# The gate of the first 1024 tokens: partial sums by GpSimd instead of TensorE

## The chip, the cores and the metric

One core of one Trainium2 chip runs the kernel. The metric is the device time of one execution in microseconds, as the median of several runs. The engines are TensorE (PE; its weight loads are PEld), VectorE (DVE), ScalarE (ACT), GpSimd (POOL) and SyncE (SP, which here only issues DMAs). "Line" and "L" numbers are lines of the kernel's source.

## The reference

The kernel computes a gated mix of an attention block and a mixture of 64 experts, for 2048 tokens of 1024 features in fp32. The gate is one number for each token, the sum over all features of x times a weight vector:

```python
def reference(A_x, A_wqkv, A_wo, B_x, B_w_q, B_k1, B_k2, B_u, B_v, gate_w):
    ...
    x = A_x
    g = _sigmoid((x * gate_w).sum(-1, keepdims=True))
    a = _A_ref(x, A_wqkv, A_wo)
    b = _B_ref(x, B_w_q, B_k1, B_k2, B_u, B_v)
    return g * a + (1 - g) * b
```

The attention needs the queries and keys, x times the first 2048 columns of wqkv. The change lies in this first stage, in the part that also sums x times gate_w.

## The kernel before

x comes transposed: features on partitions, in eight row blocks of 128 (kc from 0 to 7), tokens along the free dimension. The stage of queries and keys goes in two passes of 1024 tokens, the second half of the tokens first (pass 0), and in units of 128 output columns of queries and of keys each. x and the weights are fp32; for TensorE every operand is split in a rounded upper part (ScalarE, a copy into fp32r) and the remainder (VectorE, a subtraction), and every product is three matmuls.

The first unit of a pass is computed plainly, all the others with seven products in place of eight (Strassen's method in Winograd's form). For this x of a pass is seen as four blocks: B11 and B12 are kc 0 to 3 of the first and second 512 tokens, B21 and B22 are kc 4 to 7. In the plain unit of pass 0 (the loop over kc) each kc is loaded, split (split_x, recorded at L95 on ScalarE and L96 on VectorE) and multiplied by twelve matmuls (plain_mm, L291). Its four results lie in PSUM banks 7, 0, 1 and 2.

The code after the loop makes the sums of the seven products: x_sum (L153, VectorE) computes T1 = B12 - B11, T3 = B22 - B12, T2 = B22 - T1 and T4 = B21 - T2. Each result is written over a block that is no longer needed: T1 over B11, T3 over B12, T2 over B22, T4 over B21. x_hi and x_lo (recorded at L136 and L139) split them. The split of T3 is put where the raw B22 and T2 lay (tile xh2), so it follows x_lo of T2; that of T4 is put where B11 and B12 lay (tile xh1), so it follows x_lo of T3. evac takes a result out of a bank: a copy of its upper part, the remainder, a square with accumulation (L247, ScalarE, written in place into the bank) and two DMAs from GpSimd's queue. The squares and DMAs of one evac are put off to the next one (run_late).

unit(1) then issues the products P1, P5, P6, P2, P7, P3, P4 (product, L303), each with its bank in turn from a rotation of six (bank_at(prod_no % 6), which plain_banks sets to 3), and the adds between them (L513, VectorE). Functions put into hooks run after the product that they name. Every engine executes its instructions in the order in which the code issues them; engines wait for each other only where one needs what another writes, or writes what another still reads. Tiles with bufs=1 have one buffer: a new tile of that name waits until all readers of the old one are through, DMAs included.

The gate of pass 0 is gate_mm: a column of gw, 128x1, as the weights and x itself as the data, 256 tokens at a time, into rows 0, 32, 64 and 96 of bank 5, summed over kc in PSUM. It stands in the loop ahead of kc 4 and of kc 6, 16 matmuls each. gate_out copies the four rows into zs (a tile named u2; ScalarE, L198) and stores them in ZD by four DMAs from GpSimd's queue. Pass 1 does the same at its own place. The names u2, u4, u7 and c1 are also those of the working tiles of each unit.

Of the kernel before, what the change touches and what calls it, by code (L numbers as in the profile page):

```python
# [9 lines left out]
F32 = mybir.dt.float32  # L10
# [3 lines left out]
OP = mybir.AluOpType  # L14
# [5 lines left out]
KC = D // 128  # L20
HC = KC // 2
# [10 lines left out]
def gated_mha_peer_kernel(ctx, tc, xT, wqkv, wv, wo, wq, k12, ug, v, out):  # L32
# [8 lines left out]
    nc = tc.nc  # L41
# [23 lines left out]
    ones = const.tile([128, 32], F32, name="ones")  # L65
# [5 lines left out]
    gw = const.tile([128, KC, 1], F32, name="gw")  # L71
# [3 lines left out]
    def dma(dst, src, queue=nc.sync):  # L75
        a, b = (ap.bitcast(F32) if ap.dtype == F32R else ap for ap in (dst, src))
        return queue.dma_start(a, b)
# [37 lines left out]
    def bank_at(i):  # L115
        return ps1.tile([128, 512], F32, name=f"bk{i}")
# [3 lines left out]
    ev = Pool("ev", bufs=3)  # L120
# [5 lines left out]
    X, AW, XR, wraw = {}, {}, {}, {}  # L126
# [14 lines left out]
    def x_hi(p, name):  # L141
        X[name] = x_parts(PASS[p][name], None, xp)
        hi_of(X[name], XR[name])
# [26 lines left out]
    def load_x(p, kc, pieces=1):  # L170
        rows, t0 = slice(kc * 128, (kc + 1) * 128), TOK0[p]
        if kc < HC:
            n = 1024 // pieces
            for i in range(pieces):
                dma(XR["ra"][:, kc, i * n:(i + 1) * n], xT[rows, t0 + i * n:t0 + (i + 1) * n])
        else:
            for i, name in enumerate(("B21", "B22")):
                dma(XR[name][:, kc - HC, :], xT[rows, t0 + i * 512:t0 + (i + 1) * 512])

    def x_raw_at(kc, c):  # L180
        n, c = divmod(c, 512)
        return XR[f"B{1 + kc // HC}{1 + n}"][:, kc % HC, c:c + 256]

    pz = []

    def gate_mm(kcs):
        if kcs[0] == 0:
            pz[:] = [bank_at(5)]
        for kc in kcs:
            for q in range(4):  # L190
                nc.tensor.matmul(pz[0][32 * q:32 * q + 1, :256], gw[:, kc, :], x_raw_at(kc, 256 * q),  # L191
                                 start=(kc == 0), stop=(kc == KC - 1))

    def gate_out(p):
        zs = ev.tile([128, 512], F32, name="u2", bufs=1)
        for q in range(4):
            row = slice(32 * q, 32 * q + 1)
            nc.scalar.activation(zs[row, :256], pz[0][row, :256], AF.Copy)  # L198
            c = TOK0[p] + 256 * q
            dma(ZD[:, c:c + 256], zs[row, :256], nc.gpsimd)  # L200


    def load_w(u):
        t = wr.tile([128, 2, KC, 128], F32, name="wraw")
        for w in range(2):
            dma(t[:, w], wqkv[w * 8 + CHUNK[u]].rearrange("p (k m) -> p k m", k=KC))
        wraw[u] = raw_quarters(t)
# [73 lines left out]
    b0, prod_no = {}, [0]  # L281
# [6 lines left out]
    def plain_mm(w, n, kc, i, first=False, last=False):  # L288
        ki, k = divmod(kc, HC)
        a, b = ((0, 0), (0, 1), (1, 0))[i]  # L290
        nc.tensor.matmul(b0[w, n], AW[PLAIN[w, ki]][a][:, k, :], X[f"B{ki + 1}{n + 1}"][b][:, k, :],  # L291
                         start=first, stop=last)

    FACTORS = dict(P1=("A11", "B11"), P2=("A12", "B21"), P3=("S4", "B22"), P4=("A22", "T4"),
                   P5=("S1", "T1"), P6=("S2", "T2"), P7=("S3", "T3"))
# [22 lines left out]
    def load_wqs():  # L318
        while wq_no[0] < min(fold_no[0] + 2, 32):
            load_wq(wq_no[0])  # L320
            wq_no[0] += 1
# [53 lines left out]
    def split_w0(k0, k1):  # L375
        ki, k = divmod(k0, HC)
        for w in range(2):
            hi, lo = AW[PLAIN[w, ki]]
            split(hi[:, k:k + k1 - k0], lo[:, k:k + k1 - k0], w0[:, w, k0:k1])

    def split_x(kc):
        ki, k = divmod(kc, HC)
        for n in range(2):
            hi, lo = X[f"B{ki + 1}{n + 1}"]
            split(hi[:, k, :], lo[:, k, :], XR[f"B{ki + 1}{n + 1}"][:, k, :])
# [28 lines left out]
    for kc in range(KC):  # L414
        if kc:
            split_x(kc)
        if kc in (1, 2):
            split_w0(2 * kc, 2 * kc + 2 if kc == 1 else KC)
        if kc + 4 < KC:
            load_x(0, kc + 4)  # L420
        if kc == 3:
            load_w(1)
        if kc == 4:
            load_wqs()
        if kc == HC:
            gate_mm(range(HC))
        if kc == KC - 2:
            gate_mm(range(HC, KC))
        order = [(w, n, i) for w in range(2) for i in range(3) for n in range(2)]
        if kc == 0:  # L430
            order = [(w, n, i) for n in range(2) for pair in ((0, 2), (1,)) for w in range(2) for i in pair]
        if kc == KC - 1:
            order = [(w, n, i) for w in range(2) for n in range(2) for i in range(3)]
        for w, n, i in order:
            plain_mm(w, n, kc, i, kc == 0 and i == 0, kc == KC - 1 and i == 2)


    def plain_evac(u, w, n):
        evac(w, CHUNK[u], TOK0[u // KC] // 512 + n, b0[w, n], b0[w, n])

    hooks = {}
# [17 lines left out]
    w_lo(1, "S2")  # L459
    w_lo(1, "A12")  # L460
    plain_evac(0, 1, 0)
    gate_out(0)
    x_hi(0, "T3")
    x_lo(0, "T3")
    plain_evac(0, 0, 1)
# [6 lines left out]
    w_lo(1, "S4")  # L472
    x_lo(0, "T4")
    hooks[1, "P1"] = [(plain_evac, 0, 1, 1), (w_parts, 1, "A22"), (run_late,)]
    hooks[1, "P5"] = [(plain_evac, 0, 0, 0)]
    dma(WPD[:, :, 448:], ug.rearrange("p (k m) -> p k m", k=KC)[:, :, :64], nc.gpsimd)
    load_w(2)
    fold()
# [117 lines left out]
    plain_banks(1)  # L596
    load_wqs()
    gate_mm(range(KC))
    nxt = KC + 1

# [311 lines left out]
    class Halves:  # L912
# [9 lines left out]
                       P5=("S1", "T1"), P6=("S2", "T2"), P7=("S3", "T3"))  # L922
# [847 lines left out]
```

## Time and profile before

| | |
|---|---|
| median of 3 runs | 1818.84 us (1818.75 to 1820.33) |
| the profiled execution | 1820.62 us, span 1818.8 us |
| granted TensorE clock, mean | 0.999 |
| busy: PE, DVE, ACT, POOL | 1810.3, 1470.1, 1314.7, 230.7 us |
| the loop over kc with the gate in it | up to about 35.6 us from the span's start |
| unit 1, first product to the end of its fold | 37.5 to 58.7 us |

Times in the profile's rows are from the start of the span. A row of the timeline has the start in us, the time taken in us, the engine, the line, the operation, output <- input, how many instructions are merged in it, and in brackets how long the engine had been idle and what ended that. A row of the grouped views has the count, then busy us and mean ns of one, then the idle time ahead of them. "min/median/max" rows are ns, except for DMAs, whose time to landing is in us. A row of the table by stretches has the stretch, its length, then busy us and count for PE, PEld, DVE, ACT and POOL, the granted clock, the DMA engines' share and GB/s. The chain of waits is the work that ended last, followed back from the end.

### The profile page before, as it was taken

The page shows a single profiled execution, that of the slowest core. Times are in us where ns is not written, and L with a number is a line of the kernel's source. Part 1 is how long each engine was busy: PE and PEld are TensorE (multiplying, and loading weights), DVE is VectorE, ACT ScalarE, POOL GpSimd, SP SyncE. Part 2 cuts the span into 40 slices and gives each one's busy share as a digit, 9 for nine tenths or more (in the row PEclk, how much of TensorE's full clock was granted, in tenths as well). Part 3 has the DMA queues.
Part 4 walks back from the last instruction along what each step waited for, and adds up shares of the span by engine and source line. Part 5 has one row for each costly group of instructions (what it writes and reads, how often), then busy time and mean ns, then how long its engine had stood idle before and what let it go on. Part 6 is the DMA issues. An engine that isn't in the chain of part 4 may idle for free.

```text
span 1818.8 us, 26381 instructions
## 1 busy us (share of the span) xinstructions
PE 1810.3 (100%) x10057; PEld 1096.5 (60%) x10057; DVE 1470.1 (81%) x1273; ACT 1314.7 (72%) x1720; POOL 230.7 (13%) x355
## 2 busy tenths in 40 slices
PE   9999999999999999999999999999999999999999
PEld 6777777788888644444444444444444444447887
DVE  7865966689977888888888888888888888897874
ACT  5545644532343599999999999999999999994221
POOL 1222222244101100000000000000000000000000
PEclk9999999999999999999999999999999999999999
DMA  7888698660267878777787877888787787878641
GB/s 259 278 288 263 226 280 304 197 226 14 81 221 239 240 161 179 155 171 167 162 186 166 180 172 167 175 175 183 162 180 172 158 179 167 184 166 291 228 157 58
DMA packets 116913, 346.28 MB, mean 190 GB/s; under 512 B 16001, under 2 KB 49185, under 8 KB 95729
## 3 DMA queue, kind: packets, MB, share of 16 engines
q1 hardware_dynamic: 87320, 196.05, 36.4%
q0 software_dynamic: 28160, 146.35, 34.9%
q10 hardware_dynamic: 1304, 2.17, 0.3%
q8 instruction: 80, 1.31, 0.3%
q14 instruction: 49, 0.39, 0.1%
HBM read 171.76 MB, written 72.36 MB: 134 GB/s over the span
## 4 chain that ended last, share of the span: by engine, by line
PE 99%; DMA 0%; ACT 0%; SPq 0%; issue 0%; DVE 0%; DVEq 0%; ACTq 0%
PE ring L1322 29%; PE o L1343 26%; PE bk L303 15%; PE pa L965 7%; PE bk L965 6%; PE bk L726 5%; PE bk L291 2%; PE bk L984 2%; PE bk L342 2%; PE ring L1356 1%; PE pa L1525 1%; PE pa L1532 1%; PE bk L191 0%; DMA xh<-in_xT 0%; PE bk L359 0%; ACT P L1332 0%
## 5 line engine op out<-in xcount | busy, mean ns | idle before, releaser
L1332 ACT ACTIVATE P<-ring 128x1024 f32<-128x1024 f32 (+2 forms) x1031 | 913.0, 983 | 13.3
L1372 DVE TENSOR_TENSOR acc<-acc,P 128x2048 f32<-128x2048 f32 x319 | 731.0, 2291 | 74.5 <-ACT P L1332 48.5
L1343 PE MATMUL o<-P,V 128*32 128x512 f32 x3840 | 464.8, 599 | 0.0
L1322 PE MATMUL ring<-Q,K 98*128 98x512 f32 x1024 | 271.7, 407 | 0.1
L1322 PE MATMUL ring<-z,z 98*128 98x512 f32 x1020 | 270.4, 407 | 0.6 <-ACT accd L1332 0.6
L1322 PEld LDWEIGHTS ring<-Q,K 98*128 98x128 f32 x1024 | 182.1, 188 | 143.6 <-ACT P L1332 73.5
L1322 PEld LDWEIGHTS ring<-z,z 98*128 98x128 f32 x1020 | 181.4, 188 | 142.4 <-ACT P L1332 72.3
L1343 PEld LDWEIGHTS o<-P,V 128*32 128x32 f32 x3840 | 98.8, 109 | 223.5 <-issue 214.5
L1365 POOL DMA_DIRECT2D accd<-P x96 | 82.3, 858 | 935.4 <-ACT P L1332 327.4
L1370 DVE TENSOR_TENSOR acc<-P,P 128x2048 f32<-128x2048 f32 x32 | 73.4, 2292 | 72.6 <-ACT P L1332 72.6
L303 PE MATMUL bk<-xh,A 128*128 128x512 f32 x336 | 82.8, 396 | 0.0
L303 PE MATMUL bk<-xh,S 128*128 128x512 f32 x336 | 81.3, 393 | 0.0
L303 PE MATMUL bk<-xl,S 128*128 128x512 f32 x336 | 80.1, 391 | 0.0
L136 ACT ACTIVATE hi<-u 128x512 fp32r<-128x512 f32 x42 | 26.6, 632 | 72.2 <-DVE u L513 37.2
L303 PEld LDWEIGHTS bk<-xh,A 128*128 128x128 f32 x336 | 62.1, 188 | 23.8 <-issue 5.0
L1375 DVE TENSOR_TENSOR acc<-acc,accd 128x2048 f32<-128x2048 f32 x32 | 73.1, 2284 | 0.0
L303 PEld LDWEIGHTS bk<-xl,S 128*128 128x128 f32 x336 | 62.8, 188 | 16.3 <-issue 2.5
L965 PE MATMUL pa<-woh,acc 128*128 128x512 f32 x224 | 72.5, 389 | 0.0
L303 PEld LDWEIGHTS bk<-xh,S 128*128 128x128 f32 x336 | 62.4, 188 | 14.5 <-issue 1.7
L1332 ACT ACTIVATE accd<-ring 128x1024 f32<-128x1024 f32 (+2 forms) x64 | 62.3, 1033 | 1.8 <-PE ring L1322 1.7
L513 DVE TENSOR_TENSOR u<-u,bk 128x512 f32<-128x512 f32 x70 | 46.6, 683 | 11.3 <-PE bk L303 10.1
L730 ACT ACTIVATE xu<-bk 128x64 f32<-128x64 f32 x16 | 3.6, 222 | 61.2 <-PE bk L726 61.2
(305 smaller groups left out, 2209.7 us busy)
## 6 DMA issues: line engine op xcount, KB each, us to landing
accd<-P POOLq DMA_DIRECT2D x96, 1024.0 KB, 7.7
wqt<-in_wq SPq DMA_DIRECT2D x64, 512.0 KB
wraw<-in_wqkv SPq DMA_DIRECT2D x28, 512.0 KB
kdh<-hi POOLq DMA_DIRECT2D x32, 256.0 KB, 5.9
kdl<-lo POOLq DMA_DIRECT2D x32, 256.0 KB, 7.1
qdh<-hi POOLq DMA_DIRECT2D x32, 256.0 KB, 6.3
qdl<-lo POOLq DMA_DIRECT2D x32, 256.0 KB, 6.3
z<-kdh SPq DMA_DIRECT2D x32, 256.0 KB
```

The lines of the kernel that those rows point to most:

```text
L291: nc.tensor.matmul(b0[w, n], AW[PLAIN[w, ki]][a][:, k, :], X[f"B{ki + 1}{n + 1}"][b][:, k, :], start=first, stop=last)
L303: nc.tensor.matmul(ps, a[i][:, k, :], b[j][:, k, :], start=(k == 0 and i == j == 0), stop=(k == HC - 1 and i == 1))
L513: nc.vector.tensor_tensor(out=out, in0=a, in1=b, op=OP.add)
L726: nc.tensor.matmul(ps, x_part(a, t // 4, kc)[:, tok], b, start=first, stop=last)
L965: nc.tensor.matmul(ps, self.a[a][i][:, k, :], self.b[b][j][k], start=(not first and k == 0 and i == j == 0), stop=(k == HC - 1 and i == 1))
L1322: on_ring(nc.tensor.matmul(ring[:, i, :], K[:98, kt * 128:(kt + 1) * 128], Q[:98, qc * 512:(qc + 1) * 512], start=True, stop=True), i)
L1332: on_ring(nc.scalar.activation(P[h, kt][:, q0 * 512:(q0 + m) * 512].rearrange("p (a m) -> p a m", a=m), ring[:, i:i + m, :], AF.Exp, scale ...
L1343: nc.tensor.matmul(O[h][32 * qc:32 * qc + 32, :], Vt[g][:, kt, 32 * j:32 * j + 32], p[:, qc * 512:(qc + 1) * 512], start=(kt == 0), stop=( ...
L1365: nc.gpsimd.dma_start(ACCD[h], P[h, kt], accum_op=OP.add)
L1370: nc.vector.tensor_add(ACC[h], P[h, 0], P[h, kt])
L1372: nc.vector.tensor_add(ACC[h], ACC[h], P[h, kt])
L1375: nc.vector.tensor_add(ACC[h], ACC[h], ACCD[h])
```

## The change

The gate of pass 0 is no longer a sum of 32 small matmuls in the loop. For each kc and each half n of the tokens GpSimd multiplies the 128x512 block of x by the column of gw (tensor_scalar), and from kc 1 on adds the product to a running sum of 128x512 in fp32 (tensor_tensor). The two running sums are tiles named u4 and u7, the product is a tile named u2. Issued in the loop ahead of the matmuls of each kc, that is 16 tensor_scalar and 14 tensor_tensor. What is left is the sum over the 128 partitions: gate_fold, four matmuls with a column of ones, into the next bank of the rotation. It and gate_out are moved from the code ahead of unit 1 into unit 1, behind P5. Pass 1 still uses gate_mm.

```diff
     pz = []
 
+    def gate_acc(kc, n):
+        x = XR[f"B{1 + kc // HC}{1 + n}"][:, kc % HC, :]
+        if kc == 0:
+            pz.append(ev.tile([128, 512], F32, name=("u4", "u7")[n], bufs=1))
+            nc.gpsimd.tensor_scalar(pz[n], x, gw[:, kc, :], None, op0=OP.mult)
+        else:
+            t = ev.tile([128, 512], F32, name="u2", bufs=1)
+            nc.gpsimd.tensor_scalar(t, x, gw[:, kc, :], None, op0=OP.mult)
+            nc.gpsimd.tensor_tensor(out=pz[n], in0=pz[n], in1=t, op=OP.add)
+
...
+
+    def gate_fold():
+        parts = pz[:]
+        pz[:] = [bank_at(prod_no[0] % 6)]
+        prod_no[0] += 1
+        for q in range(4):
+            nc.tensor.matmul(pz[0][32 * q:32 * q + 1, :256], ones[:, :1], parts[q // 2][:, q % 2 * 256:q % 2 * 256 + 256],
+                             start=True, stop=True)
...
-        if kc == HC:
-            gate_mm(range(HC))
-        if kc == KC - 2:
-            gate_mm(range(HC, KC))
+        for n in (0, 1) if kc < HC else (1, 0):
+            gate_acc(kc, n)
...
     plain_evac(0, 1, 0)
-    gate_out(0)
     x_hi(0, "T3")
...
-    hooks[1, "P5"] = [(plain_evac, 0, 0, 0)]
+    hooks[1, "P5"] = [(plain_evac, 0, 0, 0), (gate_fold,), (gate_out, 0)]
```

## The prediction

> **What bounds the kernel now.** I read the page's engine shares and chain first, then the chain of waits of the first 70 us, where the change lies, then the timeline there, and last every row of the trace in which GpSimd (POOL) does arithmetic.
>
> ```profile
> PE 1810.3 (100%) x10057; PEld 1096.5 (60%) x10057; DVE 1470.1 (81%) x1273; ACT 1314.7 (72%) x1720; POOL 230.7 (13%) x355
> PE 99%; DMA 0%; ACT 0%; SPq 0%; issue 0%; DVE 0%; DVEq 0%; ACTq 0%
> ```
>
> TensorE is the bound: 99% of the chain. A microsecond that leaves its queue comes off the end, and a microsecond that it newly waits is added to the end, since it has no slack later to give it back. So the whole question is when TensorE gets through the stage around the change.
>
> ```profile
> 10.71 10.00 PE bk L291 x35
> 20.70 1.84 PE bk L191 x32
> 22.54 5.66 PE bk L291 x24
> 28.20 1.84 PE bk L191 x32
> 30.04 5.66 PE bk L291 x24
> 35.70 1.85 PE bk L342 x16
> 37.56 19.31 PE bk L303 x84
> ```
>
> L291 is the plain first unit, L191 the gate's matmuls, L342 the folds, L303 the seven products. The gate stands on the chain with 2 x 1.84 = 3.68 us. That is what the change can take from TensorE. It puts back gate_fold, four matmuls that appear as eight records: 8 x 1.84/32 = 0.46 us. Seen from TensorE alone: -3.2 us.
>
> **What VectorE does there.** The adds replace reads by TensorE with reads by GpSimd, and the blocks of x that they read are overwritten soon after by x_sum (L153): T1 goes into B11, T3 into B12, T2 into B22, T4 into B21. So these sums now wait for GpSimd. The timeline has them, and the steps that lead on to the third product, P6:
>
> ```profile
> 9.51 1.15 ACT L95 ACTIVATE xh<-xh 128x512 fp32r<-128x512 f32 x2 [2.84 <-DMA xh<-in_xT]
> 10.17 1.29 DVE L96 TENSOR_TENSOR xh<-xh,xh 128x512 fp32r<-128x512 f32 x2 [2.75 <-ACT xh L95]
> 22.58 2.29 DVE L153 TENSOR_TENSOR xh<-xh 128x2048 f32<-128x2048 f32 x1 [1.77 <-PE bk L191]
> 31.19 2.29 DVE L153 TENSOR_TENSOR xh<-xh,xh 128x2048 f32<-128x2048 f32 x1
> 36.80 2.29 DVE L139 TENSOR_TENSOR xh<-xh,xh 128x2048 fp32r<-128x2048 f32 x1
> 37.93 1.56 ACT L198 ACTIVATE u<-bk 1x256 f32<-1x256 f32 x4
> 38.58 1.98 POOL L77 DMA_DIRECT2D zd<-u  x4 [30.93 <-ACT u L198]
> 39.51 1.92 ACT L136 ACTIVATE xh<-xh 128x2048 fp32r<-128x2048 f32 x1
> 41.95 0.60 ACT L247 ACTIVATE bk<-bk 128x512 f32<-128x512 f32 x1
> 42.88 2.68 PEld L303 LDWEIGHTS bk<-xh,S 128*128 128x128 f32 x12
> 45.60 2.68 PEld L303 LDWEIGHTS bk<-xl,A 128*128 128x128 f32 x12
> 46.13 0.58 ACT L247 ACTIVATE bk<-bk 128x512 f32<-128x512 f32 x1
> 51.61 0.68 DVE L513 TENSOR_TENSOR u<-c,bk 128x512 f32<-128x512 f32 x1
> 53.76 2.68 PEld L303 LDWEIGHTS bk<-xh,A 128*128 128x128 f32 x12
> ```
>
> T1 starts at 22.58 and T2 at 31.19; the lower part of T2 (L139) ends at 39.09; P6 starts at 42.88, P2 at 45.60, P4 at 53.76. VectorE leads TensorE by 3.8 us at P6 and no more. From T2's start to the end of its lower part it takes 7.9 us without a pause: T2, the lower part of S1, T4, S2, the lower part of T2.
>
> **GpSimd's work.** It is 16 tensor_scalar and 14 tensor_tensor, each 128x512. The prices:
>
> ```profile
> 6.31 1.34 POOL L326 TENSOR_TENSOR kpad<-kraw 128x14 f32<-128x14 f32 x4 [2.94 <-DMA kraw<-in_k]
> L740 POOL TENSOR_TENSOR eq<-eq,ranks 128x512 f32<-128x512 f32 x16 | 20.6, 1289 | 14.2 <-DVE eq L739 14.2
> L324 POOL MEMSET kpad<- 128x256 f32 x1 | 0.4, 355 | 0.0
> ```
>
> The tensor_tensor has a row of its own size: 1.29 us. No tensor_scalar of GpSimd is in the trace. It has one large input; I bound it below by the memset of half the elements (0.36 us) and above by the two-input row (1.29 us), and take twice the memset, 0.71 us. The Trainium skill, GPSIMD Engine Reference, Engine selection, calls one-input work on GpSimd roughly line-rate and two-input work about half VectorE's speed; read as VectorE's pace, that would put this operation near 0.69 us, and the sum would stay within half a microsecond. No run here shows it yet.
>
> T2 needs the adds through block 7 of B22: two operations for kc 0, four each for kc 1 to 6, two for kc 7, which is 15 tensor_scalar and 13 tensor_tensor. That is 15 x 0.71 + 13 x 1.29 = 27.4 us on GpSimd, against 23.5 us between its last kpad operation (7.65) and the present T2. Already this is too long. But GpSimd isn't alone:
>
> ```profile
> L762 POOL TENSOR_TENSOR pq<-eq,p x32: 651/662/2703, 381.3 to 462.9; 128x256 f32<-128x256 f32 x32
> 381.22 2.28 DVE L96 TENSOR_TENSOR xh<-rx,xh 128x2048 fp32r<-128x2048 f32 x1
> 381.33 3.29 POOL L762 TENSOR_TENSOR pq<-eq,p 128x256 f32<-128x256 f32 x2 [0.52 <-DVE p L755]
> L750 DVE TENSOR_TENSOR eq<-eq,mm x16: 426/1058/1069, 380.0 to 460.5; 128x256 f32<-128x256 f32 x16
> 392.32 1.29 POOL L740 TENSOR_TENSOR eq<-eq,ranks 128x512 f32<-128x512 f32 x1 [0.35 <-DVE eq L739]
> 392.82 1.06 DVE L750 TENSOR_TENSOR eq<-eq,mm 128x256 f32<-128x256 f32 x1
> ```
>
> A GpSimd operation of 0.66 us that starts 0.1 us after a two-input VectorE operation takes 2.70 us and ends 0.53 us after it (381.33 + 2.70 = 384.03, against 383.50). A VectorE operation of 0.43 us that starts under a GpSimd one takes 1.06 us and ends 0.27 us after it (393.88 against 393.61). So the later one waits for the earlier; about 0.13 to 0.16 us of each is all that overlaps. In the stage of the change nearly every VectorE operation is such a two-input subtraction, so the two engines' times add.
>
> ```profile
> 7.65:31.19 23.54, 21.72 (x133) 14.93 (x132) 19.07 (x25) 12.75 (x21) 0.00 (x1) 0.93 0.89 347
> ```
>
> VectorE's busy time ahead of T2 is 19.07 us, all of it from 10.17 on. By then GpSimd has done three tensor_scalar (kc 0, and one of kc 1, whose x is there at about 9.5). Left are 12 of 0.71 and 13 of 1.29, each less the 0.16 us of overlap: 12 x 0.55 + 13 x 1.13 = 21.3 us. Whoever wins each turn, the sum is the same: T2 starts at 10.17 + 19.07 + 21.3 = 50.5 us instead of 31.19.
>
> Here the Trainium skill, SBUF — State Buffer, Who interferes with whom, goes further than the rows: it has the loser of the shared port blocked for the whole instruction. With no overlap the sum would be 25 x 0.16 = 4 us longer. The rows show the overlap, so I keep them.
>
> **From T2 to P6.** After T2 the last two GpSimd operations (B21 of kc 7) still lie ahead of T4: 0.55 + 1.13 = 1.7 us. The lower part of T2 ends at 50.5 + 7.9 + 1.7 = 60.1. gate_fold also takes a bank from the rotation of six (it was at 3 after the plain unit): P1 and P5 keep 3 and 4, gate_fold has 5, so P6 now gets bank 0, where the plain result of (1, 0) lies, and P2 gets bank 1 in place of 0. Bank 0 is free when ScalarE has squared it (L247, ended 42.55), which follows T3's upper part (39.51), which follows the lower part of T2. From L198's end (39.49) that is 3.05 us, so P6 starts at 60.1 + 3.05 = 63.2 instead of 42.88: +20.3 us. The 3.68 us of L191 are in this: TensorE only waits longer for having them off.
>
> **From P6 to the next unit.** P2 needs bank 1, squared at 46.71, which is 7.6 us after the lower part of T2: 67.7, against P6's end at 65.9. That makes the shift 22.1 us at P2 (45.60 now). Then gate_out: it moves from its place at 37.93 into P5's hook, behind the last plain evacuation. Its zs is the one buffer u2, which the first add behind P6 (L513, 51.61) writes. That add is queued behind four activations (1.56 us), four GpSimd DMAs (1.98 us) and their landing:
>
> ```profile
> DMA to landing us min/median/max: 1.5/4.0/6.6
> ```
>
> VectorE waits there with everything behind it, and the add that follows frees P5's bank 4, which P4 now takes. With the longer landing P4 would be late by up to 3 us, with the shortest not at all; I take 1 us. The other DMAs of that queue, the kdh and qdh stores of the plain results, now stand behind the adds; the results themselves come later than the adds end, so that costs nothing.
>
> Two covers remain.
>
> ```profile
> 10.19:14.88 4.69, 4.67 (x12) 3.23 (x12) 4.61 (x9) 4.12 (x9) 0.00 (x0) 0.64 1.04 408
> 58.65:80.30 21.65, 21.65 (x108) 16.50 (x104) 16.92 (x27) 12.10 (x26) 5.63 (x10) 1.00 0.81 266
> ```
>
> After its waits at the start TensorE ran at a granted clock of 0.64. Should P6 start so, its 2.7 us become 4.2, and the 1.8 us that P2 waits for its bank hide that. In unit 2 VectorE is busy for 16.92 of 21.65 us; its idle time is the cover that lets it regain its lead, and without it each unit would hand on what is missing. Sum: 20.3 + 1.8 + 1 = about 23 us.
>
> On the profiled execution that gives 1820.62 + 23 = 1843.6 us (span 1818.8 + 23); the median of the runs shown is 1818.84, 1.8 us under it. I predict 1842 us.
>
> **The rivals.**
>
> 1. The tensor_scalar costs as much as the two-input row. 13 operations of the sum are dearer by 0.58 us: +7.5 us, 1849 us. For it: the operand gw is read as well, and a reading engine may be slower than a memset. Against: nothing in the trace but the one-input memset.
>
> 2. No exclusion between the two engines for these forms. Then GpSimd runs alone: 9.5 + 13 x 0.71 + 13 x 1.29 = 35.5 for T2, +4.3 us, P6 at 35.5 + 7.9 + 3.05 = 46.5, +3.6, with the steps behind it about +6: 1825 us. For it: the trace shows the blocking for tensor_tensor against tensor_tensor, not against tensor_scalar. Against: 13 of the 28 operations are that very form.
>
> 3. Not slower: GpSimd is hidden and TensorE keeps its gain. This decides on one point: T2 must be free to start when VectorE gets there, at 31.19 - 1.77 = 29.4 (T1 no longer waits for L191). Then the lower part of T2 ends at 37.3 and P6 starts at 40.4 instead of 42.88: -2.5 us, 1816 us. Against: 13 adds at 1.29 leave 29.4 - 9.5 - 16.8 = 3.1 us for 13 tensor_scalar, 0.24 us each, under the lower bound, and with no blocking at all.
>
> **How the numbers follow.** Chances: forecast 0.73, rival 1 0.13, rival 2 0.10, rival 3 0.04. The forecast's own ends: tensor_scalar at 0.36 us takes off 13 x 0.35 = 4.6 us, no wait for u2 1 us, and a share of the operations that slip past each other some 4 us, so 1832; no overlap and the longest landing put on 4 + 2 us, so 1848. With part of rivals 1 and 2 the range is 1828 to 1853. A measurement of this kernel can tell about 0.2% (3.6 us) from no change. Faster by more than that needs more than rival 3 gives: 0.02. Within it lie most of rival 3 and the good end of rival 2: 0.05. Slower: 0.93.
>
> **What would show it.** In the changed profile: GpSimd busy without a gap from 7.6 to about 52 us; its tensor_tensor and VectorE's L96 and L139 longer than 1.29 and 0.69 us, in turns; T2 (still L153) at about 50; TensorE waiting before P5 and P6, and P6's wait ended by ScalarE's square; the add u2 waiting on zd. From the third unit on, the same spacing as before. I am wrong if VectorE's rows keep 0.69 us while GpSimd runs, if T2 starts before 40, or if the shift at the first product of unit 2 differs much from the shift at the end.

## The result, and the profile after

The changed kernel takes 1859.91 us (median of four runs, 1859.08 to 1861.33) against 1818.91 us: 1.0223 times as long, 95% interval 1.0211 to 1.0235. It is slower, as forecast, but by 41 us in place of 23, beyond the range. The profiled execution took 1861.33 us with a span of 1859.6, 40.8 us over that of before. Lines have moved: the products are L321 now, the folds L360, the squares L265, the adds L528; GpSimd's tensor_scalar are L190 and L193, its tensor_tensor L194.

The page after, first rows:

```profile
span 1859.6 us, 26316 instructions
PE 1816.1 (98%) x10001; PEld 1098.7 (59%) x10001; DVE 1480.3 (80%) x1273; ACT 1314.4 (71%) x1720; POOL 288.1 (15%) x385
```

TensorE is busy for 5.8 us more than before (1816.1 against 1810.3) in a span that is 40.8 us longer: it waits. Who waited for whom in the first 100 us (total, times, longest):

```profile
DVE xh L153 <- POOL u L193: 22.2, 3, 17.8
PE bk L321 <- DVE S L139: 21.0, 1, 21.0
DVE u L528 <- DMA zd<-u: 5.3, 1, 5.3
PE bk L321 <- ACT bk L265: 5.2, 1, 5.2
PE bk L321 <- DVE u L528: 1.8, 1, 1.8
```

The sums T1, T3 and T2 wait for GpSimd, TensorE waits for what is queued behind T2 on VectorE, then for bank 0's square, then for the add that waits for the gate's stores. These are the waits that the prediction named. The timeline, TensorE and VectorE, with the steps that the prediction showed of before:

```profile
32.04 1.92 PE L360 MATMUL bk<-wqt,kpad 128*32 128x512 f32 x16
58.88 2.29 DVE L153 TENSOR_TENSOR xh<-xh,xh 128x2048 f32<-128x2048 f32 x1 [17.84 <-POOL u L193]
64.31 2.29 DVE L153 TENSOR_TENSOR x<-x,xh 128x2048 f32<-128x2048 f32 x1 [1.46 <-POOL u L193]
68.21 2.28 DVE L139 TENSOR_TENSOR xh<-xh,xh 128x2048 fp32r<-128x2048 f32 x1
73.62 5.49 PE L321 MATMUL bk<-xh,S 128*128 128x512 f32 x12 [5.23 <-ACT bk L265]
78.91 3.37 PE L321 MATMUL bk<-xl,A 128*128 128x512 f32 x12
89.53 4.61 PE L321 MATMUL bk<-xh,A 128*128 128x512 f32 x12 [1.81 <-DVE u L528]
94.07 1.92 PE L360 MATMUL bk<-wqt,kpad 128*32 128x512 f32 x16
```

The same view of before, at the fold behind the plain unit, at P6 and at the fold behind unit 1:

```profile
35.63 1.92 PE L342 MATMUL bk<-wqt,kpad 128*32 128x512 f32 x16
43.10 2.88 PE L303 MATMUL bk<-xh,S 128*128 128x512 f32 x12
56.80 1.92 PE L342 MATMUL bk<-wqt,kpad 128*32 128x512 f32 x16
```

The gain of the change is there: the fold behind the plain unit starts at 32.04 us, 3.6 us earlier than its 35.63. Then T2 starts 27.7 us late (58.88 against 31.19), P6 30.7 us late (73.62 against 42.88, the start of its weight loads in the kernel before, from which the prediction counts; its first matmul there was at 43.10), and the fold behind unit 1 37.3 us late (94.07 against 56.80). The router's first product is still 37.3 us late, the end 40.8.

What GpSimd's operations cost. First the groups between 41.1 and 57 us, while VectorE stands still (one of the six additions began just before that); then two of the timeline from the stage in which VectorE works, and VectorE's own beside them:

```profile
L194 POOL TENSOR_TENSOR u<-u,u 128x512 f32<-128x512 f32 x6 | 7.6, 1270 | 0.5
L193 POOL TENSOR_SCALAR u<-x,gw 128x512 f32<-128x512 f32 x3 | 4.7, 1562 | 0.3
...
22.27 2.40 POOL L193 TENSOR_SCALAR u<-xh,gw 128x512 f32<-128x512 f32 x1
24.76 1.33 POOL L194 TENSOR_TENSOR u<-u,u 128x512 f32<-128x512 f32 x1
...
22.65 0.68 DVE L96 TENSOR_TENSOR xl<-x,xl 128x512 fp32r<-128x512 f32 x1
23.25 1.09 DVE L96 TENSOR_TENSOR xl<-xh,xl 128x512 fp32r<-128x512 f32 x1
24.27 0.68 DVE L96 TENSOR_TENSOR xl<-x,xl 128x512 fp32r<-128x512 f32 x1
24.87 1.77 DVE L96 TENSOR_TENSOR xl<-xh,xl 128x512 fp32r<-128x512 f32 x1
```

Undisturbed, the addition takes 1.26 to 1.27 us, as forecast, and the multiplication by the gate's column 1.56 us, where 0.71 was taken and 1.29 was thought the most. GpSimd's chain up to the last read of B22 is 15 tensor_scalar and 12 additions, for T2 starts as the fifteenth tensor_scalar ends; the addition behind that one reads the product and not x. By the undisturbed prices the chain is 15 x 1.56 + 12 x 1.26 = 38.5 us. It ran from 7.8 to 58.8, which is 51 us: about 2.2 us are gaps between operations, and by 10.4 us its operations were longer while VectorE worked.

### The profile page after: what moved, and what is told of

It reads as the page before. It is cut to its first block, busy times and chain, and to the rows that moved or that the text cites. A ratio compares the mean times of both kernels' runs of the same rounds, so it can differ in the third digit from the quotient of the medians.

```text
span 1859.6 us, 26316 instructions
## 1 busy us (share of the span) xinstructions
PE 1816.1 (98%) x10001; PEld 1098.7 (59%) x10001; DVE 1480.3 (80%) x1273; ACT 1314.4 (71%) x1720; POOL 288.1 (15%) x385
## 3 DMA queue, kind: packets, MB, share of 16 engines
q1 hardware_dynamic: 87320, 196.05, 35.7%
q8 instruction: 79, 1.29, 0.3%
## 4 chain that ended last, share of the span: by engine, by line
PE 89%; DMA 3%; issue 2%; DVE 1%; ACT 0%; POOL 0%; SPq 0%; DVEq 0%; POOLq 0%; ACTq 0%
PE ring L1337 27%; PE o L1358 25%; PE bk L321 14%; PE pa L980 7%; PE bk L741 5%; PE bk L999 2%; PE bk L980 2%; PE bk L360 2%; PE ring L1371 1%; DMA accd<-P 1%; PE bk L309 1%; PE pa L1540 1%; PE pa L1547 1%; DMA xl<-in_wo 1%; DMA t1l<-xl 0%
## 5 line engine op out<-in xcount | busy, mean ns | idle before, releaser
L321 PE MATMUL bk<-xl,S 128*128 128x512 f32 x336 | 82.0, 397 | 22.3 <-DVE S L139 21.0
L321 PE MATMUL bk<-xh,A 128*128 128x512 f32 x336 | 84.7, 402 | 4.4 <-DVE A L139 2.6
L321 PE MATMUL bk<-xh,S 128*128 128x512 f32 x336 | 83.9, 402 | 5.2 <-ACT bk L265 5.2
L321 PEld LDWEIGHTS bk<-xl,S 128*128 128x128 f32 x336 | 63.7, 191 | 39.7 <-DVE S L139 21.5
L321 PEld LDWEIGHTS bk<-xh,A 128*128 128x128 f32 x336 | 63.0, 191 | 29.4 <-issue 6.7
L321 PEld LDWEIGHTS bk<-xh,S 128*128 128x128 f32 x336 | 63.9, 193 | 20.8 <-ACT bk L265 5.7
L528 DVE TENSOR_TENSOR u<-u,bk 128x512 f32<-128x512 f32 x70 | 46.6, 683 | 10.4 <-DMA wpd<-u 5.1
L980 PEld LDWEIGHTS pa<-woh,acc 128*128 128x128 f32 x224 | 42.0, 188 | 8.7
```

The costliest lines, as they stand in the source:

```text
L321: nc.tensor.matmul(ps, a[i][:, k, :], b[j][:, k, :], start=(k == 0 and i == j == 0), stop=(k == HC - 1 and i == 1))
L528: nc.vector.tensor_tensor(out=out, in0=a, in1=b, op=OP.add)
L980: nc.tensor.matmul(ps, self.a[a][i][:, k, :], self.b[b][j][k], start=(not first and k == 0 and i == j == 0), stop=(k == HC - 1 and i == 1))
```

## The experiments

Two theories were put against each other. **Length**: T2 is late because it waits for GpSimd's chain, and the chain is long by its own operations. **Sum**, the prediction's: the two engines shut each other out, so their times add. Behind T2, **tail** (the moved steps cost time of their own) stood against **head** (they don't).

**What the operations cost: leave out one kind.** Without the multiplications of kc 1 to 7:

```diff
-            t = ev.tile([128, 512], F32, name="u2", bufs=1)
-            nc.gpsimd.tensor_scalar(t, x, gw[:, kc, :], None, op0=OP.mult)
-            nc.gpsimd.tensor_tensor(out=pz[n], in0=pz[n], in1=t, op=OP.add)
+            nc.gpsimd.tensor_tensor(out=pz[n], in0=pz[n], in1=x, op=OP.add)
```

> The changed kernel with x added unweighted: the tensor_scalar of kc 1 to 7 is left out, so GpSimd issues 2 tensor_scalar and 14 tensor_tensor. Theory 'length' (T2 starts when GpSimd's own chain is through, mostly because a tensor_scalar takes 1.56 us): 2 x 1.56 + 13 x 1.26 and gaps make 20.7 us, with some 8 us of blocking T2 starts near 37 us, P6 6 to 8 us later than before; 1828 us. Rival 'sum' (the port makes both engines' times add): T2 at 10.2 + 19.1 + 14.7 = 44 us, 1838 us.

Measured: 1840.61 us, 1.0116 times before (1.0099 to 1.0133). Its counterpart has the multiplications only:

```diff
-            nc.gpsimd.tensor_tensor(out=pz[n], in0=pz[n], in1=t, op=OP.add)
+            nc.gpsimd.tensor_scalar(pz[n], x, gw[:, kc, :], None, op0=OP.mult)
```

(with t and its multiplication dropped as above.)

> The changed kernel with 16 tensor_scalar and no additions: each product overwrites the one before, so only kc 7 is left in the sum. It is the counterpart of e3_nomul (14 tensor_tensor, T2 at 44.0 us with VectorE never waiting for GpSimd). If a tensor_scalar shares the port for only a part of its 1.56 us ('short hold'): VectorE's splits stretch less than there, T2 near 37 us although GpSimd's own chain is longer; about 1832 us. If it holds the port for all its time ('sum'): 10.2 + 19.1 + 13 x 1.4 = 47.5 us for T2; about 1843 us.

Measured: 1837.9 us, 1.0099 (1.0082 to 1.0116). VectorE's splits (groups) and T1 and T2 (timeline), first with the additions only, then with the multiplications only:

```profile
L96 DVE TENSOR_TENSOR xl<-xh,xl 128x512 fp32r<-128x512 f32 x4 | 6.0, 1498 | 0.0
35.37 2.28 DVE L153 TENSOR_TENSOR xh<-xh 128x2048 f32<-128x2048 f32 x1
43.97 2.28 DVE L153 TENSOR_TENSOR xh<-xh,xh 128x2048 f32<-128x2048 f32 x1
```

```profile
L96 DVE TENSOR_TENSOR xl<-xh,xl 128x512 fp32r<-128x512 f32 x4 | 3.1, 781 | 0.0
22.47 2.69 DVE L153 TENSOR_TENSOR xh<-xh 128x2048 f32<-128x2048 f32 x1
39.22 2.77 DVE L153 TENSOR_TENSOR xh<-xh,xh 128x2048 f32<-128x2048 f32 x1 [6.53 <-POOL u L192]
```

This is the clearest pair. Beside additions a split takes 1.50 us instead of 0.69 in the mean (three of the four take 1.76 to 1.78, the last, behind GpSimd's end, 0.68), T1 comes at 35.4 us although GpSimd never makes it wait, and T2 at 44.0, the sum's number: for two-input operations on both sides the times add. Beside multiplications a split takes 0.78 us and T1 comes at 22.47 without a wait. Before, it came at 22.58, after 1.77 us of waiting for the gate's matmuls; so VectorE lost about 1.7 us here. T2 at 39.2 waits for GpSimd's chain: there it is length. The chain with multiplications is the longer one, and still T2 comes sooner. The total of this kernel, 1837.9 us, is no verdict: it lies midway between the 1832 and the 1843 us that were expected, and while P6 is 7.6 us late by its first matmul, the fold behind unit 1 is 14.4.

**The multiplication in another form.** As a two-input operation, and with a constant:

```diff
-            nc.gpsimd.tensor_scalar(t, x, gw[:, kc, :], None, op0=OP.mult)
+            nc.gpsimd.tensor_tensor(out=t, in0=x, in1=gw[:, kc, :].to_broadcast([128, 512]), op=OP.mult)
```

> The changed kernel with the 14 products of kc 1 to 7 as tensor_tensor with the gate's column broadcast along the row, in place of tensor_scalar. 'Length': the two-input form takes 1.26 us against 1.56 us, 13 of them ahead of T2 make 4 us; about 1856 us. Rival 'sum': the two-input form holds the port for longer of its time than the tensor_scalar, VectorE is blocked for more; 1860 us or more.

Measured: 1854.77 us, 1.0192 (1.0175 to 1.0209); T2 at 53.37, 5.5 us sooner than in the changed kernel. The two-input form is the cheaper one here, as length has it; the one product that ran while VectorE stood still took 1.04 us:

```profile
52.30 1.04 POOL L193 TENSOR_TENSOR u<-xh,gw 128x512 f32<-128x512 f32 x1
```

VectorE was slowed more: T1 came at 35.7 in place of 28.1. T2 waited only 3.4 us for GpSimd, so VectorE's stretched work and GpSimd's chain ended nearly together, and this run doesn't separate the theories by T2.

```diff
-            nc.gpsimd.tensor_scalar(t, x, gw[:, kc, :], None, op0=OP.mult)
+            nc.gpsimd.tensor_scalar(t, x, 0.05, None, op0=OP.mult)
```

(the same in the line of kc 0.)

> The changed kernel with a constant as the factor in place of the column of gw, so the weights are left out and tensor_scalar reads no second operand. If the pointer to the column is what makes it 1.56 us: near 0.7 us, T2 near 48 us, about 1848 us. If the operation itself takes that long on GpSimd: 1.5 us, 1860 us.

Measured: 1856.31 us, 1.0198 (1.0181 to 1.0215). The undisturbed pair at its start took 1.49 us each instead of 1.56. The column of gw isn't what makes the operation long. The total is nearer to the 1860 us of that theory than to 1848, but 3.6 us under the changed kernel: T2 came at 54.95, 3.9 us sooner, and while VectorE worked most of these operations took 1.81 us where most of those with the column took 2.40.

**Only the mutual exclusion, no waiting for GpSimd.** What the two engines exclude each other from is called the port in the expectations. The first attempt gave GpSimd a tile of its own, with fold and store left out and other numbers stored early:

```diff
+        t = pz[0]
+        nc.gpsimd.tensor_scalar(t, t, gw[:, kc, :], None, op0=OP.mult)
+        if kc:
+            nc.gpsimd.tensor_tensor(out=t, in0=t, in1=t, op=OP.add)
...
+    for q in range(4):
+        dma(ZD[:, TOK0[0] + 256 * q:TOK0[0] + 256 * q + 256], xT[q:q + 1, :256], nc.gpsimd)
     dma(kraw, k12.rearrange("p (a e) -> p a e", a=2), nc.gpsimd)
```

> As the kernel without fold and store, but the 30 GpSimd operations run on one tile of their own (u7) and read no x: nothing of x_sum waits for them, only the port is still shared. The gate of pass 0 is left out with that. 'Length' (the port costs VectorE some 1.4 times its time while GpSimd runs, as the changed kernel's rows between 12 and 27 us show): the lower part of T2 ends near 50 us, P6 about 7 us later than before; 1826 us. Rival 'sum' (the times add): the lower part of T2 ends near 70 us, 1845 us.

Measured: 1848.73 us, 1.0156 (1.0139 to 1.0173), and for another reason than either. Its waits:

```profile
DVE lo L139 <- DMA kdl<-lo: 23.3, 1, 23.3
ACT hi L136 <- DMA kdh<-hi: 22.2, 1, 22.2
```

GpSimd also issues the stores of queries and keys. They stood behind its arithmetic until 75 us, and VectorE and ScalarE waited for the buffers. The second attempt sends these stores over SyncE's queue, stores the other numbers late, and stops GpSimd after kc 5:

```diff
-            late.append((dma, dst[128 * c:128 * c + 128, n * 512:(n + 1) * 512], t, nc.gpsimd))
+            late.append((dma, dst[128 * c:128 * c + 128, n * 512:(n + 1) * 512], t,
+                         nc.sync if c < 2 <= n else nc.gpsimd))
...
-        for n in (0, 1) if kc < HC else (1, 0):
+        for n in (0, 1) if kc < 6 else ():
```

> What e5_detach meant to show, without its two faults: GpSimd works on a tile of its own and reads no x (12 tensor_scalar and 10 tensor_tensor, so that it ends near 50 us); the stores of the first two units go over SyncE's queue, so that none stands behind GpSimd's arithmetic; fold and store are left out. Only the port is shared. 'Length' (what holds T2 back in the changed kernel is that it waits for GpSimd's chain; the port alone costs VectorE little of its lead): the lower part of T2 ends near 45 us, P6 3 to 5 us later than before; 1823 us. Rival 'sum' (each GpSimd operation takes its whole time from VectorE): the lower part of T2 ends near 60 us; 1838 us.

Measured: 1834.62 us, 1.0083 (1.0067 to 1.01). Where the theories differ it is length: T2 starts at 35.75 and its lower part ends at 45.7; but for its first matmul (44.3) P6 starts at 45.8, 2.9 us after the 42.88 of before. The additions here read one tile twice and take 1.04 us undisturbed (the first attempt's, while VectorE stood still), not 1.26, so this kernel may spare VectorE a little. GpSimd pays instead; the group of its multiplications has a mean of 2.93 us:

```profile
L192 POOL TENSOR_SCALAR u<-u,gw 128x512 f32<-128x512 f32 x12 | 35.2, 2932 | 1.2
35.75 3.12 DVE L153 TENSOR_TENSOR xh<-xh,xh 128x2048 f32<-128x2048 f32 x1
```

The total missed its 1823 us: 2.9 us at P6 had become 9.5 at the router and 12.6 at the end. The moved stores are the difference to the other kernels there, and were not tested by themselves.

**The tail.** The gate's rows in u7, which is needed one product later, in place of u2:

```diff
-        zs = ev.tile([128, 512], F32, name="u2", bufs=1)
+        zs = ev.tile([128, 512], F32, name="u2" if p else "u7", bufs=1)
```

> The changed kernel with one edit: the gate's four rows are copied into the tile u7 in place of u2, so the first add behind P6 no longer waits for the four stores of the gate (5.3 us of VectorE's waiting in the changed kernel). Theory 'tail' (the steps moved into unit 1 cost time of their own, behind the wait for GpSimd): P4 loses its 1.8 us wait and most of the 1.7 us by which its slow clock lengthened it; about 1856 us. Rival 'head' (all that counts is when GpSimd lets T2 start, VectorE's later waits are hidden): no change, 1860 us.

Measured: 1857.17 us, 1.021 (1.0193 to 1.0227), 2.7 us less than the changed kernel. P4 no longer waits, and the fold behind unit 1 comes at 90.06 instead of 94.07 us. Without gate_fold and gate_out, first with the early stores of above:

> The changed kernel without gate_fold and gate_out of pass 0: the sum over partitions and its store are left out (other numbers are stored early in their place), the 30 GpSimd operations stay. The bank rotation is then that of before, and no store holds u2. 'Tail': P6 starts when the lower part of T2 is there, near 70.5 us, not 3 us later, and the first product of unit 2 comes about 7 us earlier than in the changed kernel; 1852 us. 'Head': only the 0.6 us of the fold's own matmuls and the store's wait go; 1857 us or more.

Measured: 1857.7 us, 1.0208 (1.0191 to 1.0225). The early stores delayed kraw on GpSimd's queue, and with it the whole chain: T2 at 63.70. The second version stores other numbers in their place too, but late and from SyncE (fill_zd):

```diff
-    hooks[1, "P5"] = [(plain_evac, 0, 0, 0), (gate_fold,), (gate_out, 0)]
+    hooks[1, "P5"] = [(plain_evac, 0, 0, 0), (fill_zd,)]
```

> As e2_nofold (fold and store of the gate of pass 0 left out), but the numbers stored in their place are stored late and from SyncE's queue, so that nothing on GpSimd's queue is ahead of the 30 operations that wasn't there in the changed kernel. 'Tail': T2 at 58.9 us as in the changed kernel, P6 near 70.5 us in place of 73.6 us, the fold behind unit 1 some 7 us earlier than its 94.1 us; 1853 us. 'Head': 1858 us.

Measured: 1853.48 us, 1.0184 (1.0167 to 1.0201), 6.4 us less than the changed kernel. The timeline has the same T2 and the expected steps behind it (the first matmul of P6 comes at 69.0, the other eleven with the lower part of T2):

```profile
58.89 2.29 DVE L153 TENSOR_TENSOR xh<-xh,xh 128x2048 f32<-128x2048 f32 x1 [17.86 <-POOL u L193]
70.56 4.75 PE L325 MATMUL bk<-xh,S 128*128 128x512 f32 x11 [1.04 <-DVE xh L139]
87.26 1.92 PE L364 MATMUL bk<-wqt,kpad 128*32 128x512 f32 x16
```

The tail is real: the moved steps and the bank that the fold takes cost some 6 to 7 us of the 41, about 3 of them the wait for the stores.

**A smaller share.** GpSimd for kc 0 to 3, or for kc 0 and 1; TensorE does the others in bank 5, the fold adds to it, and fold and store stand at the store's old place:

```diff
-        for n in (0, 1) if kc < HC else (1, 0):
-            gate_acc(kc, n)
+        if kc < HC:
+            gate_acc(kc, 0)
+            gate_acc(kc, 1)
+        if kc == KC - 2:
+            sums = pz[:]
+            pz[:] = [bank_at(5)]
+            gate_mm(range(HC, KC))
...
     plain_evac(0, 1, 0)
+    gate_fold(sums)
+    gate_out(0)
```

> The changed kernel with GpSimd adding kc 0 to 3 only; kc 4 to 7 stay 16 matmuls on TensorE ahead of kc 6, in bank 5; the fold adds to that bank, and fold and store stand where the store stood before. 'Length': 8 tensor_scalar and 6 tensor_tensor, T3 starts at about 33 us as in the changed kernel, T2 near 39.5 us, P6 near 47.6 us instead of 42.9; about 1823 us. Rival 'sum': T2 near 42 us and 1827 us. If half of it could be hidden: 1817 us.

Measured: 1830.94 us, 1.0061 (1.0045 to 1.0078). That is beyond both theories. T3 came as expected (33.2), T2 at 40.5, between the 39.5 of length and the 42 of the sum; but the fold now waited 2.6 us for GpSimd ahead of the products, and P6 waited for gate_out to free bank 5: 48.84 in place of 47.6. With kc 0 and 1 only:

> The changed kernel with GpSimd adding kc 0 and 1 only (4 tensor_scalar, 2 tensor_tensor, through at about 18 us), kc 2 to 7 on TensorE as before, the fold in bank 5 and the store at its place of before. TensorE is rid of 0.92 us and gets 0.46 us. If the work is hidden once it is through before T1 (22.6 us): 1819 us, no difference that can be measured. If even so few operations cost VectorE its lead through the port: 1821 to 1824 us.

Measured: 1822.25 us, 1.0013 (1.0003 to 1.0022). T1 to T4 wait for nothing of GpSimd's and P6 starts 0.5 us early, its first matmul at 42.57 against 43.10. VectorE's lead is shorter all the same (T2 at 31.83 in place of 31.19), and the square of a later bank takes the gain back; the timeline:

```profile
51.19 3.02 PE L318 MATMUL bk<-xl,S 128*128 128x512 f32 x12 [0.30 <-ACT bk L262]
56.86 1.92 PE L357 MATMUL bk<-wqt,kpad 128*32 128x512 f32 x16
```

The fold behind unit 1 is at 56.86, against 56.80 before; the 1 to 2 us that the total is over before arise behind it and were not traced. Even a quarter of the work brings nothing, and none of the runs points to a version that beats the kernel before.

**Mere delay.** The kernel before, with VectorE kept busy ahead of T2:

```diff
+    idle = ev.tile([128, 512], F32, name="u7", bufs=1)
+    nc.vector.memset(idle, 1.0)
+    for i in range(46):
+        nc.vector.tensor_tensor(out=idle, in0=idle, in1=idle, op=OP.max)
     x_sum(0, "T2")
```

> The kernel before (gate wholly on TensorE, no GpSimd arithmetic) with nothing added but time: one memset and 46 tensor_tensor of 128x512 on a tile of VectorE's own, queued ahead of T2, about 28 us. T2 then starts near 59 us as in the changed kernel, and P6 some 24 us later than before. If the changed kernel's loss is that T2 is late and nothing of GpSimd's: the fold behind unit 1 comes 27 us later than before, and a few us more are lost far behind, as in the changed kernel (3.5 us from unit 2 to the end); 1849 us. If the late losses need GpSimd's operations or the moved store: 1846 us.

Measured: 1852.55 us, 1.0178 (1.0161 to 1.0195). The 46 operations, each of which needs the result of the one before, took 33.4 us and not 28, so T2 came at 65.12:

```profile
65.12 2.28 DVE L153 TENSOR_TENSOR xh<-xh,xh 128x2048 f32<-128x2048 f32 x1
73.46 3.01 PE L303 MATMUL bk<-xh,S 128*128 128x512 f32 x12 [0.77 <-ACT u L198]
90.11 1.92 PE L342 MATMUL bk<-wqt,kpad 128*32 128x512 f32 x16
```

A T2 that is 33.9 us late makes the fold 33.3 and the end 33.9 us late: the delay of T2 alone, with no GpSimd, costs itself almost whole. In the changed kernel a T2 that is 27.7 us late costs 37.3 at the same fold; the rest there is GpSimd's last two operations ahead of T4, the later bank of P6 and the tail.

## Why the prediction was wrong

The mechanism was right in its outline: T2 waits for GpSimd, the blocks can't be overwritten sooner, TensorE pays. Most signs to look for came as named: GpSimd busy almost without a gap, T2 late, P6's wait ended by the square, the add waiting for zd. Two of the signs of being wrong came as well, one of them in part: while GpSimd ran, some of VectorE's splits kept their 0.68 us (the rows at 22.65 and 24.27 above), and the shift grew from 37.3 us at the first product of unit 2 to 40.8 at the end.

**The step that failed is the price of tensor_scalar.** It was taken at 0.71 us, twice a memset, with the two-input row of 1.29 us as its upper end. It measured 1.56 us, over that end, so the bound was none: nothing in the trace excluded that a one-input operation is slower than a two-input one. Rival 1 had the direction and not the size. T2 came at 58.9 and not 50.5: 8.4 us. No run has a tensor_scalar of 0.71 us, so that the price makes up the 8.4 us is worked out and not shown; the kernel with the product as a tensor_tensor of about 1.04 us had T2 5.5 us sooner. The Trainium skill, GPSIMD Engine Reference, Engine selection, has one-input work roughly at line rate and two-input work about twice as slow as VectorE. Here VectorE's 128x512 takes 0.69 us, GpSimd's addition 1.27 (in agreement) and its tensor_scalar 1.56 (not), and the measurement decides.

**The sum over both engines was half wrong, and hidden by that.** With the measured prices it gives 10.17 + 19.07 + 12 x 1.40 + 13 x 1.11 = 60.5 us, close to 58.88, but that is luck, for the profile shows another course: VectorE was through by 41 us and stood still for 17.8 while GpSimd went on alone. It also counts one addition too many ahead of T2, 13 where T2 waits behind 12: 1.1 us, which hid as much of the miss. Addition against subtraction excludes, as the rows of before had shown; in the kernel with additions only the blocked splits took 1.76 to 1.78 us. A tensor_scalar holds VectorE back for only a part of its time: beside it splits took 0.78 us where 0.69 is their own. The Trainium skill, SBUF — State Buffer, Who interferes with whom, has a VectorE instruction with two SBUF inputs contend with a GpSimd instruction that reads SBUF, and the later of two that contend fully blocked. The additions agree but for the small overlap that the prediction read; the tensor_scalar does not, and the measurement decides. That the blocking had been seen for one pair of forms only was said in rival 2, and not used in the sum.

**From T2 to P6** went as worked out, with 2 us more: the lower part of T2 ended 11.6 us after T2's start and not 9.6, since T4 waited 1.46 us for GpSimd's last block and the two short operations on either side of T4 took 1.76 us each in place of 0.69, beside GpSimd's additions of 3.37. The bank that the fold takes cost what was forecast: P6 3.1 us behind T2's lower part, against 3.05.

**The tail was taken at 2.8 us and was 6.6** (37.3 less 30.7). The stores held u2 for longer (5.3 us of VectorE's waiting, 1.8 of TensorE's), and the clock was costed at nothing with P2's wait as cover. The stretches of P6 and of P4, with the granted clock as the third figure from the end:

```profile
41.10:58.88 17.78, 0.73 (x2) 0.30 (x2) 0.00 (x1) 0.00 (x0) 16.74 (x12) 0.53 0.00 0
73.62:78.90 5.28, 5.28 (x12) 4.13 (x13) 4.58 (x6) 4.53 (x8) 1.51 (x3) 0.50 0.53 183
89.53:94.07 4.54, 4.54 (x12) 3.32 (x12) 4.37 (x8) 2.48 (x6) 1.08 (x2) 0.62 0.30 121
```

After waits of 5.2 and 1.8 us TensorE ran at 0.50 and 0.62 of its clock: 5.28 and 4.54 us for products of 2.72. The first was partly covered, the second, which followed the wait for the stores, by nothing. A wait of that length alone doesn't decide it: in the kernel with additions only P4 waited 1.95 us and ran at a granted clock of 1.00. No run shows what does.

**Left open: 3.5 us lost behind unit 2**, where nothing was forecast: 37.3 us late at the router's start, 39.6 at the first attention head that is loaded in its turn, 40.8 at the end. The waits behind it are of 1 us each (for a split of the values, for a sum of the attention). The kernel with mere delay lost 0.6 us there, the one without fold and store 1.0, the one with the gate's rows in u7 2.7, so lateness alone doesn't seem to do it. But these are differences of single profiled executions, and executions of one kernel lie up to 3.7 us apart (the kernel before, 1818.4 to 1822.2 us): a part of the 3.5 us can be that spread. No run isolates the cause.

Of the 17.8 us that were missing, 8.4 thus arise ahead of T2 (the price, less what the sum counted too much), 2.0 between T2 and its lower part, 3.8 in the tail, and 3.5 are open.

## What to carry to other kernels

Work that is moved to an idle engine must end before its input is overwritten: compare its whole chain, from rows of the very same operation, with that moment, not with the engine's idle time. Where no such row exists, the nearest ones are no bounds; measure the operation first. And follow what the moved step takes with it: a bank, a buffer's name and a place in a queue cost 6 us here, and an engine's DMAs wait behind its arithmetic.

## What the runs showed of the hardware

- GpSimd's tensor_scalar on 128x512 fp32 takes 1.56 us with a column as factor and 1.49 with a constant; its tensor_tensor takes 1.26 to 1.27 us on two tiles, and 1.04 where both inputs are the same tile.
- Against VectorE's two-input operations the two forms behave differently: beside tensor_tensor a VectorE operation of 0.69 us took 1.50 in the mean of a group of four, beside tensor_scalar 0.78. GpSimd itself was stretched in both, its tensor_scalar to 2.93 us on average where VectorE never stood still.
- 46 operations of VectorE that each read the result of the one before took 0.73 us each; independent ones of this size start every 0.60 us.
